# Attention and two feed-forward layers in one kernel: the conversion of w_in started earlier, cut into two steps and spread over more units

## The chip, the cores and the metric

One core of a Trainium2 chip runs the whole kernel. The metric is the device time of one execution in microseconds (us). Five engines work side by side, each through its own queue, strictly in order: PE (TensorE: matrix products and transposes), ACT (ScalarE), DVE (VectorE), POOL (GpSimd) and SP (here only the issuer of most transfers). An engine that waits for something holds everything that is queued behind it.

## The reference

```python
def _attn_ref(q, k, v, f):                      # q, k, v: (4, 8, 576, 64); f: (4, 8, 576)
    scores = scale * np.matmul(q, k.transpose(0, 1, 3, 2))
    cum = np.cumsum(np.log(np.clip(f, 0.0001, 1.0)), axis=-1)
    decay = cum[:, :, :, None] - cum[:, :, None, :]
    scores = np.where(causal, -1000000000.0, scores + decay)
    attn = softmax(scores)                      # with 1e-09 added to the sum
    return np.matmul(attn, v)

def _moe_ref(x, w_in, w_out):                   # w_in: 512 x 2048, w_out: 2048 x 512
    h = x @ w_in
    g = h * np.tanh(softplus(h))
    return g @ w_out

def _moe2_ref(x, w1, w2, w3, w_out):
    h = np.maximum(np.maximum(x @ w1, x @ w2), x @ w3)
    return h @ w_out

def reference(**kwargs):
    x = attn_out.transpose(0, 2, 1, 3).reshape(2304, 512)
    return _moe2_ref(_moe_ref(x, ...), ...)
```

The weights come as 64-bit floats; the kernel reads them as pairs of 32-bit words and makes 32-bit floats of them.

## The kernel before

**Attention.** The 32 heads are worked in 16 pairs, four to a batch element, counted here from 0 (pair 6 is the third of the second batch element). Each pair is cut into two units by rows of queries: unit 0 holds the rows 0 to 255, unit 1 the rows 256 to 575. `load` (L256) lets SP fetch q, k and the decay rows of a pair, two pairs ahead; `prep` (L304) turns q and k on PE (`tr`, L315 and L316) and copies them out of PSUM on ACT (`kT`, `qT`, `q`, L317 to L320); POOL masks the decay rows (`cb`, L298 and L302). `scores` (L341) multiplies on PE (`sc`, L339), adds the decay and finds the row minimum on DVE (`P<-sc`, L393, with `mn`), exponentiates on ACT (L399) and scales each row by its sum: the reciprocal on DVE (`rr`, L360 and L361), the product on POOL (L363). `av` (L407) runs two units later: PE turns P (`pp`, L438), ACT and DVE copy it out in turn (`TA`, `TB`, L442 and L444), PE multiplies with v (L418), and `split` writes the result as a high half `xh` (ACT, L134) and a low half `xl` (DVE, L140). The banks of PSUM for `tr` and `pp` are three in all (tag `ps`), so a bank that waits to be copied out holds back the next `pp`.

**w_in.** `load_w_in` (L201) makes the weights of the first feed-forward layer ready while attention runs. It has 16 chunks of 256 x 256, numbered here 0 to 15; two make one of the eight tiles `wi`. For a chunk SP fetches 512 KB into `wr` (L149; four buffers), and `convert` (L154) runs five steps on it: the absolute value of the upper word on ACT (`wt<-wr`, L159), a clip on POOL (`wt<-wt`, L163), and three steps on DVE (L166, L169, L173), of which the last two read `wr` again. `split` then writes the high half on ACT (`wi<-wt`, L134) and the low half on POOL (`wi<-wt,wi`, L140). `wt` has two buffers.

**What sets the order.** The program is written as generators that a main loop (from L540 on) advances one unit at a time; a scheduler then orders the instructions of each engine by priority and by times it estimates. Attention stands under `tc.high_priority(AHEAD)` with AHEAD = 3000; the conversion has no such rank and fills gaps. `queued(last)` holds an instruction behind another on its queue. In the main loop `na` counts units, and this line says how many steps of the conversion follow each:

```python
for _ in range(2 if 2 <= na <= 9 else na == 1):
    next(wgen, None)
```

The first step only fetches; after it, two chunks follow each of the units 2 to 9.

**The products with w_in.** `h_steps` (L505) multiplies blocks of 512 tokens with a `wi` (`h`, L184 to L186: three matmuls for each product, hi by hi, hi by lo, lo by hi). It has the lowest rank and is what PE does between the pieces of attention. After attention the second weight matrix and the second layer follow; the change does not touch them.

Of the kernel before, what the change touches and what calls it, by code (L numbers as in the profile page):

```python
# [12 lines left out]
I32 = mybir.dt.int32  # L13
AF = mybir.ActivationFunctionType
ALU = mybir.AluOpType
# [10 lines left out]
F32_MIN_AS_HIGH_HALF = struct.unpack("<f", struct.pack("<I", 0x38100000))[0]  # L26
F32_MAX_AS_HIGH_HALF = struct.unpack("<f", struct.pack("<I", 0x47EFFFFF))[0]
# [5 lines left out]
BLK = 256  # L33
BLK2 = 512
LEAD = 2
EDGE = 352


# [27 lines left out]
def tile_decay_attention__mish_ff__max3_ff(  # L66
# [16 lines left out]
    nc = tc.nc  # L83
# [10 lines left out]
    edge = ctx.enter_context(tc.tile_pool(name="edge", bufs=1, side="right"))  # L94
    edge.tile([128, EDGE // 4], F32, name="edge")
    at = ExitStack()
# [35 lines left out]
    def split(dst_hi, dst_lo, src, eng_hi, eng_lo):  # L132
        if eng_hi == "act":
            nc.scalar.activation(dst_hi, src, AF.Copy)  # L134
        elif eng_hi == "pool":
            nc.gpsimd.tensor_scalar(dst_hi, src, 1.0, 1.0, op0=ALU.mult, op1=ALU.mult)
        else:
            nc.vector.tensor_copy(dst_hi, src)
        eng = nc.gpsimd if eng_lo == "pool" else nc.vector
        return eng.tensor_tensor(out=dst_lo, in0=src, in1=dst_hi, op=ALU.subtract)  # L140

    pace, on_act, on_dve = [], [], []

    def fetch(pool, src, bufs):

        m, n = src.shape[0] // 128, src.shape[1]
        r = pool.tile([128, m, n, 2], I32, name="wr", tag="wr", bufs=bufs)
        with queued(pace):
            nc.sync.dma_start(  # L149
                r.rearrange("p m n w -> p m (n w)"), src.bitcast(I32).rearrange("(m p) w -> p m w", p=128)  # L150
            )
        return r

    def convert(pool, r, bufs=None, abs_eng="dve"):  # L154

        t = pool.tile([128, r.shape[1], r.shape[2]], F32, name="wt", tag="wt", bufs=bufs)
        lo, hi, ti = r[:, :, :, 0], r[:, :, :, 1], t.bitcast(I32)
        if abs_eng == "act":
            nc.scalar.activation(t, hi.bitcast(F32), AF.Abs)  # L159
        else:  # L160
            nc.vector.tensor_scalar(ti, hi, 0x7FFFFFFF, None, op0=ALU.bitwise_and)
        eng = nc.gpsimd if abs_eng == "act" else nc.vector
        eng.tensor_scalar(  # L163
            t, t, F32_MIN_AS_HIGH_HALF, F32_MAX_AS_HIGH_HALF, op0=ALU.max, op1=ALU.min
        )
        nc.vector.tensor_scalar(  # L166
            ti, ti, 3, 0x3FFFFFF8, op0=ALU.logical_shift_left, op1=ALU.bitwise_and
        )
        nc.vector.scalar_tensor_tensor(  # L169
            out=ti, in0=hi, scalar=-0x40000000, in1=ti,  # L170
            op0=ALU.bitwise_and, op1=ALU.bitwise_or,
        )
        nc.vector.scalar_tensor_tensor(  # L173
            out=ti, in0=lo, scalar=29, in1=ti,
            op0=ALU.logical_shift_right, op1=ALU.bitwise_or,
        )
        return t

    def queued(last):
        return tc.issue_after(last[-1].ins) if last else ExitStack()  # L180
# [15 lines left out]
    wst = top.enter_context(tc.tile_pool(name="wst", bufs=2))  # L196
# [3 lines left out]

    def load_w_in():  # L201
        jobs = [(fp, c) for fp in range(NFP) for c in range(0, KD, 2)]
        raws = []
        for k, (fp, c) in enumerate(jobs):
            for f_, c_ in jobs[len(raws):k + 3]:
                raws.append(fetch(wst, moe_w_in[c_ * 128:(c_ + 2) * 128, f_ * 256:f_ * 256 + 256], 4))
            if k == 0:
                yield
            t = convert(wst, raws[k], abs_eng="act")
            split(wi[fp][:, 0, c:c + 2], wi[fp][:, 1, c:c + 2], t, "act", "pool")  # L210
            if c + 2 == KD:
                loaded.add(fp)
            yield

    x = {}
# [25 lines left out]
    raws = [[ap_.tile([128, 640], F32, name=f"raw{c}{i}") for c in "qk"] for i in range(2)]  # L241
# [99 lines left out]
    def scores(J, g):  # L341


        P = {}
        u = count["unit"]
        count["unit"] += 1
        sm = sums[u % 4]
        mn = aw.tile([128, 6], F32, name="mn", bufs=4)
        rr = aw.tile([128, 5], F32, name="rr", bufs=4)
        tiles = [(h, qt) for qt in ((0, 1) if g == 0 else (2, 3)) for h in range(2)]  # L350
        if g == 1:
            tiles.append((None, 4))
        made = []
        col = 0

        def scale_rows(part):

            cs = slice(part[0], part[-1] + 1)
            with tc.high_priority(400):
                nc.vector.tensor_scalar(rr[:, cs], sm[:, cs], 1e-9, None, op0=ALU.add)  # L360
                nc.vector.reciprocal(rr[:, cs], rr[:, cs])  # L361
                for ci in part:
                    nc.gpsimd.tensor_scalar(made[ci], made[ci], rr[:, ci:ci + 1], 1.0, op0=ALU.mult, op1=ALU.mult)  # L363

        for ci, (h, qt) in enumerate(tiles):
            wd = (qt + 1) * 128 if qt < 4 else S
            Pt = aw.tile([128, wd], F32, name=f"P{qt}_{h}", bufs=LEAD)
            made.append(Pt)
            if h is None:
                P[4] = Pt  # L370
            else:
                P[h, qt] = Pt
            cb = decay(J, h, qt)
            if h is None:
                cb = [cb[:, n:n + 1] for n in range(2)]
            else:
                cb = [cb]
            s0 = 128 if qt == 1 else 0
            if not h and qt != 1:
                count["sc"] += 1  # L380
                pair = (aps if count["sc"] % 2 or not eps else eps[0]).tile([128, 2, 512], F32, name="sc", bufs=1)
                for n in range(2):
                    if h is None:
                        score_mm(J, h, qt, pair[:, n, :288], 288 * n, 288)
                    else:
                        score_mm(J, n, qt, pair[:, n, :wd], 0, wd)
                if qt == 0:
                    for n in range(2):
                        score_mm(J, n, 1, pair[:, n, 128:384], 0, 256)
            for pi, (c0, w) in enumerate([(0, wd)] if qt < 4 else [(0, 288), (288, 288)]):  # L390
                sc = pair[:, h or pi, s0:s0 + w]
                like = lambda t: t.rearrange("p (a c) -> p a c", a=cb[pi].shape[1])
                nc.vector.tensor_tensor_reduce(  # L393
                    out=like(Pt[:, c0:c0 + w]), in0=like(sc), in1=cb[pi],
                    scale=-scale, scalar=(3e38 if pi == 0 else mn[:, col - 1:col]),
                    op0=ALU.add, op1=ALU.min, accum_out=mn[:, col:col + 1],
                )
                col += 1
            nc.scalar.activation(  # L399
                Pt, Pt, AF.Exp, scale=-1.0, bias=mn[:, col - 1:col], accum_out=sm[:, ci:ci + 1],  # L400
            )
            if ci == 1:
                scale_rows([0, 1])
        scale_rows(list(range(2, len(tiles))))
        return P

# [54 lines left out]
    def attention():  # L461
# [9 lines left out]
        pend = []  # L471
        for n in range(len(units) + LEAD):
            if n == 6 + LEAD:
                eps.clear()
                early.close()
                eps_h.append(sa.enter_context(tc.tile_pool(name="hps", bufs=2, space=PSUM, reuse_waits="tile")))
            if n < len(units):
                ji, g = units[n]
                pend.append((J[ji], g, scores(J[ji], g)))
            if n >= LEAD:  # L480
                unit = pend.pop(0)
# [5 lines left out]
            if n < len(units) and g == (ji == 0) and ji + 1 < len(jobs):  # L487
                prep(J[ji + 1])
            if n >= LEAD:
                next(rest, None)  # L490
# [14 lines left out]
    def h_steps():  # L505
# [3 lines left out]
        for i, j in order:  # L509
# [28 lines left out]
            yield i  # L538

    wgen = load_w_in()  # L540
    attn = attention()
    steps = h_steps()
    credit, na = 0.0, 0
    while True:

        with tc.high_priority(AHEAD):
            done = next(attn, None)
        if done is None:
            break

        na += 1
        for _ in range(2 if 2 <= na <= 9 else na == 1):
            next(wgen, None)
        if len(loaded) == NFP and not x4:
            top.close()
            x4.append(top.enter_context(tc.tile_pool(name="x4", bufs=1)))
            x4[0].tile([128, (864 - EDGE) // 4], F32, name="gap")
        credit += RATE
        while credit >= 1.0:
            credit -= 1.0  # L560
            if next(steps, None) is None:
                credit = 0.0
# [274 lines left out]
    for t0 in (BLK2, BLK2 + 2 * HALF):  # L837
        hh = [hp2.tile([128, 2 * HALF], F32R, name=f"hh{c}") for c in range(NF2)]
        hl = [hp2.tile([128, 2 * HALF], F32R, name=f"hl{c}") for c in range(NF2)]
        for p in range(3):  # L840
            fs = slice(p * 128, p * 128 + 128)
            for m in range(3):
                S = []
                for k in range(4):
                    t = sst.tile([128, 2, 2, 128], F32R, name="s")
# [88 lines left out]
```

## Time and profile before

| what | value |
|---|---|
| median of 3 runs | 902.48 us (902.36 to 904.47) |
| the profiled execution's own time | 902.15 us |
| its span | 900.4 us |
| mean granted TensorE clock | 0.992 of 2.4 GHz |
| busy: PE, DVE, ACT, POOL | 97%, 56%, 45%, 26% of the span |

Shares of the span hide that the stages differ. The profile cuts the span into 40 slices of 22.5 us: POOL is busy for 8 to 9 tenths in the slices 3 to 5 and again for 8 tenths in slice 7, and for 3 tenths or less from slice 8 on. PE is at 9 tenths or more from slice 7 to slice 39. A row of the timeline gives the start, the length, the engine, the line, the operation and, in brackets, how long the engine sat idle before it and what ended that. Lines (L163) are those of the kernel before.

### The profile page before, as it was taken

The numbers are of one execution on the slowest core, as the hardware profiler recorded it, in microseconds if no ns is written. First come the engines' busy times: TensorE is split into PE (matmuls) and PEld (weight loads), VectorE is DVE, ScalarE is ACT, GpSimd is POOL, SyncE is SP. The second block draws the span as 40 slices with busy tenths as digits, with TensorE's granted clock in tenths as the row PEclk, the third lists the DMA queues.
The fourth block names the chain that finished last, engine by engine and source line by source line (L and its number), as shares of the span: only waits on it lengthen the run. The fifth ranks groups of instructions, "written<-read, shape, count | busy, mean of one in ns | idle before, by whom it ended". The sixth has DMA issues, their size and how long they took to land.

```text
span 900.4 us, 13933 instructions
## 1 busy us (share of the span) xinstructions
PE 873.3 (97%) x4800; PEld 704.8 (78%) x4800; DVE 504.9 (56%) x1186; ACT 401.7 (45%) x913; POOL 231.6 (26%) x317
## 2 busy tenths in 40 slices
PE   6898989999999999999999999999999999999998
PEld 3565756777777777889888888889888999889986
DVE  3688676354544433991367566675865556524540
ACT  4687656555555432443464455453433223312211
POOL 3689968333222210000020000000121323013310
PEclk8989999999999999999999999999999999999999
DMA  7886654444433115863456666673499443334401
GB/s 184 227 220 178 198 164 128 123 127 119 125 113 86 59 59 178 284 229 128 136 182 210 224 201 217 205 240 104 160 364 324 144 139 106 123 94 129 131 27 65
DMA packets 125030, 145.25 MB, mean 161 GB/s; under 512 B 64736, under 2 KB 78048, under 8 KB 124960
## 3 DMA queue, kind: packets, MB, share of 16 engines
q1 hardware_dynamic: 105856, 102.41, 38.9%
q10 hardware_dynamic: 16416, 27.79, 8.3%
q0 software_dynamic: 2688, 14.16, 4.3%
q8 instruction: 38, 0.62, 0.3%
q14 instruction: 32, 0.26, 0.1%
HBM read 102.83 MB, written 41.49 MB: 160 GB/s over the span
## 4 chain that ended last, share of the span: by engine, by line
PE 88%; POOL 3%; DMA 3%; DVE 2%; ACT 2%; issue 2%; SPq 1%; ACTq 0%; POOLq 0%; DVEq 0%
PE y L184 7%; PE y L185 7%; PE y L186 7%; PE h L184 6%; PE h L186 6%; PE h L185 6%; PE q L185 6%; PE q L186 6%; PE q L184 6%; PE sc L339 6%; PE av L418 4%; PE pp L438 4%; PE o L184 3%; PE o L185 3%; PE o L186 3%; PE g L184 2%
## 5 line engine op out<-in xcount | busy, mean ns | idle before, releaser
L184 PE MATMUL h<-xh,wi 128*128 128x512 f32 (+1 forms) x320 | 122.0, 383 | 0.6 <-DVE he L528 0.4
L185 PE MATMUL h<-xl,wi 128*128 128x512 f32 (+1 forms) x320 | 120.1, 375 | 1.8 <-DVE xl L140 1.8
L186 PE MATMUL h<-xh,wi 128*128 128x512 f32 (+1 forms) x320 | 120.1, 375 | 0.0
L185 PE MATMUL y<-gl,wo 128*128 128x512 f32 (+1 forms) x320 | 117.7, 368 | 0.0
L186 PE MATMUL y<-gh,wo 128*128 128x512 f32 (+1 forms) x320 | 117.5, 368 | 0.0
L184 PE MATMUL y<-gh,wo 128*128 128x512 f32 (+1 forms) x320 | 106.4, 369 | 0.0
L668 DVE TENSOR_TENSOR gl<-g,gh 128x512 fp32r<-128x512 f32 x72 | 49.9, 695 | 86.3 <-ACT gh L667 86.2
L363 POOL TENSOR_SCALAR P<-P,rr 128x128 f32<-128x128 f32 (+3 forms) x128 | 73.7, 589 | 85.1 <-DVE rr L361 51.2
L399 ACT ACTIVATE P<-P,mn 128x128 f32<-128x128 f32 (+3 forms) x128 | 70.6, 553 | 40.0 <-DVE mn L393 39.9
L661 ACT ACTIVATE g<-g 128x512 f32<-128x512 f32 x72 | 45.4, 633 | 88.7 <-DMA g<-h_d 85.7
L184 PEld LDWEIGHTS h<-xh,wi 128*128 128x128 f32 x320 | 60.2, 189 | 17.4 <-issue 3.2
L185 PEld LDWEIGHTS h<-xl,wi 128*128 128x128 f32 x320 | 60.4, 189 | 13.5 <-DVE xl L140 2.2
L186 PEld LDWEIGHTS h<-xh,wi 128*128 128x128 f32 x320 | 60.4, 189 | 11.4 <-issue 1.8
L185 PEld LDWEIGHTS y<-gl,wo 128*128 128x128 f32 x320 | 60.3, 189 | 10.1
L184 PEld LDWEIGHTS y<-gh,wo 128*128 128x128 f32 x320 | 60.2, 188 | 10.1
L186 PEld LDWEIGHTS y<-gh,wo 128*128 128x128 f32 x320 | 60.2, 188 | 10.0
L339 PE MATMUL sc<-kT,qT 64*128 64x128 f32 (+3 forms) x256 | 51.0, 500 | 4.4 <-DVE mn L393 4.0
L860 DVE TENSOR_TENSOR u<-q,p 128x448 f32<-128x448 f32 x36 | 22.4, 621 | 58.1 <-PE q L186 58.1
L438 PE MATMUL pp<-ident,P 128*128 128x128 f32 x320 | 49.7, 284 | 4.3 <-ACT qT L317 3.9
L531 ACT ACTIVATE he<-h 128x512 f32<-128x512 f32 x56 | 33.2, 593 | 44.6 <-PE h L186 41.5
L438 PEld LDWEIGHTS pp<-ident,P 128*128 128x128 f32 x320 | 37.2, 143 | 20.0 <-issue 5.8
L667 ACT ACTIVATE gh<-g 128x512 fp32r<-128x512 f32 x72 | 44.4, 620 | 9.4 <-PE y L186 8.9
(141 smaller groups left out, 1846.4 us busy)
## 6 DMA issues: line engine op xcount, KB each, us to landing
g<-h_d SPq DMA_DIRECT2D x72, 256.0 KB, 3.1
s<-s_d SPq DMA_DIRECT2D x72, 256.0 KB, 2.9
h_d<-he ACTq DMA_DIRECT2D x56, 256.0 KB, 2.8
wr<-in_moe_w_out_dram SPq DMA_DIRECT2D x22, 512.0 KB, 4.6
wr<-in_moe_w_dram SPq DMA_DIRECT2D x24, 384.0 KB, 3.8
s_d<-sk POOLq DMA_DIRECT2D x12, 768.0 KB, 5.8
cb<-cum_d SPq DMA_DIRECT2D x32, 256.0 KB, 4.1
wr<-in_moe_w_in_dram SPq DMA_DIRECT2D x16, 512.0 KB, 4.2
```

The source lines that it names most:

```text
L184: nc.tensor.matmul(ps, wh, xh, start=start, stop=False, skip_group_check=True)
L185: nc.tensor.matmul(ps, wh, xl, start=False, stop=False, skip_group_check=True)
L186: return nc.tensor.matmul(ps, wl, xh, start=False, stop=stop, skip_group_check=True)
L339: nc.tensor.matmul(dst, lhs, J["k"][rows, c0:c0 + w], start=True, stop=True, skip_group_check=True)
L363: nc.gpsimd.tensor_scalar(made[ci], made[ci], rr[:, ci:ci + 1], 1.0, op0=ALU.mult, op1=ALU.mult)
L399: nc.scalar.activation(Pt, Pt, AF.Exp, scale=-1.0, bias=mn[:, col - 1:col], accum_out=sm[:, ci:ci + 1],)
L418: last = nc.tensor.matmul(acc[(U, L)[h], off:off + w], J["vs"][:, n * 64:n * 64 + 64], T[:, at[h]:at[h] + w], start=(kt, off) == first, st ...
L438: turn = nc.tensor.transpose(pp[:, n * 128:n * 128 + 128], Pt[:, k0:k0 + 128], ident)
L531: nc.scalar.activation(he, h, AF.Copy)
L661: nc.scalar.activation(g, g, AF.Mish)
L667: on_act[:] = [nc.scalar.activation(gh, g, AF.Copy)]
L668: on_dve[:] = [nc.vector.tensor_tensor(out=gl, in0=g, in1=gh, op=ALU.subtract)]
```

## The change

`convert` is cut into two: `convert` now ends after the clip when the absolute value is on ACT, and a new `join` holds the three steps on DVE. `load_w_in` keeps a list `begun`: a step of the generator starts chunk k (absolute value, clip) and then finishes chunk k - 1 (`rest`: join, split). The clip is held behind the last scaling of a unit so far (`on_scale`), the join behind the last score of a unit so far (`on_score`). The first fetch gets the rank 2950, just below attention. The steps are spread anew: the fetch follows unit 1, nothing follows unit 2, and one step follows each of the units 3 to 18.

```diff
+LAG = 1
...
         eng = nc.gpsimd if abs_eng == "act" else nc.vector
-        eng.tensor_scalar(
-            t, t, F32_MIN_AS_HIGH_HALF, F32_MAX_AS_HIGH_HALF, op0=ALU.max, op1=ALU.min
-        )
+        with queued(on_scale if abs_eng == "act" else []):
+            eng.tensor_scalar(
+                t, t, F32_MIN_AS_HIGH_HALF, F32_MAX_AS_HIGH_HALF, op0=ALU.max, op1=ALU.min
+            )
+        return t if abs_eng == "act" else join(r, t)
+
+    def join(r, t):
+
+        lo, hi, ti = r[:, :, :, 0], r[:, :, :, 1], t.bitcast(I32)
...
     def load_w_in():
         jobs = [(fp, c) for fp in range(NFP) for c in range(0, KD, 2)]
-        raws = []
-        for k, (fp, c) in enumerate(jobs):
-            for f_, c_ in jobs[len(raws):k + 3]:
-                raws.append(fetch(wst, moe_w_in[c_ * 128:(c_ + 2) * 128, f_ * 256:f_ * 256 + 256], 4))
-            if k == 0:
-                yield
-            t = convert(wst, raws[k], abs_eng="act")
+        raws, begun = [], []
+
+        def rest(k, r, t):
+            fp, c = jobs[k]
+            with queued(on_score):
+                join(r, t)
             split(wi[fp][:, 0, c:c + 2], wi[fp][:, 1, c:c + 2], t, "act", "pool")
             if c + 2 == KD:
                 loaded.add(fp)
+
+        for k in range(len(jobs)):
+            for f_, c_ in jobs[len(raws):k + 3]:
+                with tc.high_priority(2950) if len(raws) < 1 else ExitStack():
+                    raws.append(fetch(wst, moe_w_in[c_ * 128:(c_ + 2) * 128, f_ * 256:f_ * 256 + 256], 4))
+            if k == 0:
+                yield
+            begun.append((k, raws[k], convert(wst, raws[k], abs_eng="act")))
+            if len(begun) > LAG:
+                rest(*begun.pop(0))
+            yield
+        while begun:
+            rest(*begun.pop(0))
             yield
...
-                    nc.gpsimd.tensor_scalar(made[ci], made[ci], rr[:, ci:ci + 1], 1.0, op0=ALU.mult, op1=ALU.mult)
+                    on_scale[:] = [nc.gpsimd.tensor_scalar(made[ci], made[ci], rr[:, ci:ci + 1], 1.0, op0=ALU.mult, op1=ALU.mult)]
...
-                nc.vector.tensor_tensor_reduce(
+                score = nc.vector.tensor_tensor_reduce(
...
+            if ci == len(tiles) - 1:
+                on_score[:] = [score]
...
-        for _ in range(2 if 2 <= na <= 9 else na == 1):
+        for _ in range((0,1,0,1,1,1,1,1,1,1,1,1,1,1,1,1,1,1,1)[na] if na < 19 else 0):
             next(wgen, None)
```

No instruction is added or removed in the conversion itself; what changes is where each stands on its queue. Three places matter below. In the names `wr` and `wt` are the raw and the converted chunk, `P_0` and `P_1` the two heads' probabilities, numbers at the end only tell tiles apart.

The first is ACT's queue where the conversion begins. Before, with chunk 0 and chunk 1:

```order
L317 ACTIVATE kT<-tr 128x512
L399 ACTIVATE P_0_728,sums_176<-P_0_728,mn 128x384
L159 ACTIVATE wt<-wr 128x512
L399 ACTIVATE P_1_734,sums_176<-P_1_734,mn 128x384
L159 ACTIVATE wt<-wr 128x512
L317 ACTIVATE qT<-tr 128x512
L318 ACTIVATE kT<-tr 128x64
L320 ACTIVATE q_1_193<-tr 64x64 x2
L134 ACTIVATE xh_450<-av 128x256
```

Now, with the two absolute values of chunk 1 and chunk 2 (chunk 0 stands 16 rows earlier, and its high half is the first row here):

```order
L135 ACTIVATE wi_152<-wt 128x512
L418 ACTIVATE P_0_663,sums_176<-P_0_663,mn 128x384
L465 ACTIVATE TA<-pp 128x512
L418 ACTIVATE P_1_669,sums_176<-P_1_669,mn 128x384
L336 ACTIVATE kT<-tr 128x512
L160 ACTIVATE wt<-wr 128x512
L135 ACTIVATE xh_415<-av 128x256
L418 ACTIVATE P_0_676,sums_176<-P_0_676,mn 128x512
L160 ACTIVATE wt<-wr 128x512
L418 ACTIVATE P_1_682,sums_176<-P_1_682,mn 128x512
L337 ACTIVATE kT<-tr 128x64
L339 ACTIVATE q_1_193<-tr 64x64 x2
```

So two absolute values stand here as before, now those of the second and third transfer, and the copies `kT` 128x64 and `q` stand behind both.

The second is SP's queue at the loads of the third pair (pair 2), now:

```order
L280 DMA rawq_179<-in_q_dram 128x4x64 x2
L284 DMA rawq_179<-in_q_dram 64x2x64
L294 DMA cb<-cum_d 128x2x256
L150 DMA wr<-in_moe_w_in_dram 128x2x512
L294 DMA cb<-cum_d 128x2x256
L297 DMA cb_367<-cum_d 64x576 x2
```

Before, four fetches of w_in stood together after the loads of pair 4 (`DMA wr<-in_moe_w_in_dram 128x2x512 x4`). Now one stands here, and a group of four, the transfers of chunks 1 to 4, stands where the group stood.

The third is DVE's queue in pair 6, from the scores of 384 columns to those of 512. Before:

```order
L166 TENSOR_SCALAR wt<-wt 128x512
L140 TENSOR_TENSOR xl_1473<-av,xh_1472 128x128
L169 SCALAR_TENSOR_TENSOR wt<-wr,wt 128x512
L173 SCALAR_TENSOR_TENSOR wt<-wr,wt 128x512
L393 ISA P_0_1631,mn<-sc,cb 128x384
...
L166 TENSOR_SCALAR wt<-wt 128x512
...
L361 RECIPROCAL rr<-rr 128x2
L140 TENSOR_TENSOR xl_594<-av,xh_593 128x256
L166 TENSOR_SCALAR wt<-wt 128x512
L169 SCALAR_TENSOR_TENSOR wt<-wr,wt 128x512
L393 ISA P_0_1644,mn<-sc,cb 128x512
```

Now:

```order
L176 SCALAR_TENSOR_TENSOR wt<-wr,wt 128x512
L141 TENSOR_TENSOR xl_1407<-av,xh_1406 128x128
L180 SCALAR_TENSOR_TENSOR wt<-wr,wt 128x512
L412 ISA P_0_1585,mn<-sc,cb 128x384
...
L379 TENSOR_SCALAR rr<-sums_176 128x2
L380 RECIPROCAL rr<-rr 128x2
L141 TENSOR_TENSOR xl_549<-av,xh_548 128x256
L412 ISA P_0_1598,mn<-sc,cb 128x512
```

One chunk's steps still stand ahead of the scores of 384 columns; the two that stood between those and the scores of 512 columns are gone from there.

## Rows read from the trace of the kernel before

**Rows 1.** Windows: stretch, length, busy PE, PEld, DVE, ACT, POOL (instructions), clock, DMA share, GB/s.
```profile
67.50:90.00 22.50, 19.23 (x169) 13.13 (x165) 19.00 (x51) 15.94 (x46) 21.14 (x22) 1.00 0.65 178
90.00:112.50 22.50, 22.26 (x145) 16.01 (x141) 14.82 (x41) 13.85 (x36) 21.46 (x25) 1.00 0.68 199
112.50:135.00 22.50, 18.10 (x122) 13.11 (x123) 17.49 (x34) 12.89 (x30) 15.67 (x14) 1.00 0.53 163
135.00:157.50 22.50, 21.22 (x118) 15.11 (x115) 14.59 (x44) 14.02 (x38) 18.45 (x21) 1.00 0.45 129
157.50:180.00 22.50, 22.50 (x146) 15.99 (x146) 8.93 (x37) 11.50 (x33) 6.82 (x14) 1.00 0.40 123
```

**Rows 2.** PE's timeline on both sides of its longest wait in attention.
```profile
40.97 0.60 PE L438 MATMUL pp<-ident,P 128*128 128x128 f32 x4
45.48 1.11 PE L438 MATMUL pp<-ident,P 128*128 128x128 f32 x4 [3.90 <-ACT qT L317]
```

**Rows 3.** ACT's timeline over the same stretch.
```profile
41.85 0.66 ACT L159 ACTIVATE wt<-wr 128x512 f32<-128x512 f32 x1 [3.42 <-DMA wr<-in_moe_w_in_dram]
42.42 0.60 ACT L399 ACTIVATE P<-P,mn 128x384 f32<-128x384 f32 x1
...
44.27 0.67 ACT L159 ACTIVATE wt<-wr 128x512 f32<-128x512 f32 x1 [1.16 <-DMA wr<-in_moe_w_in_dram]
...
45.42 0.45 ACT L320 ACTIVATE q<-tr 64x64 f32<-64x64 f32 x2
45.89 0.38 ACT L134 ACTIVATE xh<-av 128x256 fp32r<-128x256 f32 x1
46.17 0.71 ACT L399 ACTIVATE P<-P,mn 128x512 f32<-128x512 f32 x1
```

**Rows 4.** The chain that ended last, from 36 to 46 us: start, length, what.
```profile
37.62 6.63 DMA wr<-in_moe_w_in_dram
```

**Rows 5.** SP's timeline: the last load of pair 2's q, and the first of w_in.
```profile
20.82 0.61 SPq L265 DMA_DIRECT2D rawq<-in_q_dram  x1
...
36.99 2.63 SPq L149 DMA_DIRECT2D wr<-in_moe_w_in_dram  x4
```

**Rows 6.** The tile wr: its 16 transfers, from issue to landing.
```profile
DMA to landing us min/median/max: 3.6/4.2/7.9
```

**Rows 7.** PE's window with the low clock, columns as in rows 1, PE alone.
```profile
45.20:52.00 6.80, 6.53 (x27) 0.50 0.91 223
```

**Rows 8.** PE's waits from 100 to 157 us: total us, times, longest.
```profile
PE sc L339 <- DVE mn L393: 4.9, 4, 2.1
PE av L418 <- ACT TB L444: 0.8, 1, 0.8
```

**Rows 9.** PE's timeline, the two longest of those waits.
```profile
115.86 1.13 PE L339 MATMUL sc<-kT,qT 64*128 64x512 f32 x4 [1.49 <-DVE mn L393]
...
124.48 0.75 PE L339 MATMUL sc<-kT,q 128*128 128x288 f32 x2 [2.11 <-DVE mn L393]
```

**Rows 10.** DVE's timeline ahead of them.
```profile
112.40 0.83 DVE L166 TENSOR_SCALAR wt<-wt 128x512 int32<-128x512 int32 x1 [2.00 <-POOL wt L163]
...
114.68 0.55 DVE L393 CUSTOM_DVE_ANT_0 P<-sc,cb 128x384 f32<-128x384 f32 x1
...
121.30 1.18 DVE L166 TENSOR_SCALAR wt<-wt 128x512 int32<-128x512 int32 x1
122.51 0.69 DVE L169 SCALAR_TENSOR_TENSOR wt<-wr,wt 128x512 int32<-128x512 int32 x1
123.12 0.68 DVE L393 CUSTOM_DVE_ANT_1 P<-sc,cb 128x512 f32<-128x512 f32 x1
```

**Rows 11.** POOL's timeline in pair 6: four scalings, two clips, one low half.
```profile
108.75 1.62 POOL L363 TENSOR_SCALAR P<-P,rr 128x128 f32<-128x128 f32 x4
110.45 3.81 POOL L163 TENSOR_SCALAR wt<-wt 128x512 f32<-128x512 f32 x2
115.50 1.27 POOL L140 TENSOR_TENSOR wi<-wt,wi 128x512 fp32r<-128x512 f32 x1 [1.25 <-ACT wi L134]
```

More of the change, by code (lines that the diff above doesn't have):

```diff
@@ L140, in split @@
         return eng.tensor_tensor(out=dst_lo, in0=src, in1=dst_hi, op=ALU.subtract)
-    pace, on_act, on_dve = [], [], []
+    pace, on_act, on_dve, on_score, on_scale = [], [], [], [], []
     def fetch(pool, src, bufs):
```

## The prediction

> **What bounds the kernel now.** I read the windows first. From 157.5 us on PE is busy without a gap (22.50 of 22.50) while POOL has fallen to 6.82 [rows 1]; ahead of that, while w_in is converted, PE lacks 3.27 us in 67.5 to 90, 0.24, 4.40 and 1.28 us in the next three stretches, and POOL works 21.14, 21.46, 15.67 and 18.45 of each 22.50 us [rows 1]. So the end is set by PE, and what the change can win is PE's idle time in the stretch in which attention and the conversion share the engines. PE's work itself stays the same.
>
> Then PE's timeline: the longest wait in attention is 3.90 us, up to 45.48, and was ended by ACT's copy `qT` [rows 2]. ACT's timeline says why ACT was late: it stood 3.42 us until 41.85 and 1.16 us until 44.27 at the absolute values of chunks 0 and 1, for their transfers [rows 3]. The chain of waits runs through the same place: 6.63 us of the transfer that lands at 44.25 [rows 4]. Behind that wait PE's granted clock is 0.50, its lower level of 1.2 GHz, from 45.2 to 52.0 us, with 6.53 us of work in it [rows 7]; at 2.4 GHz this work would be about half, so the spell costs some 3.3 us more.
>
> Then PE's waits from 100 to 157 us: 4.9 us in four waits for scores to be read by DVE, and one of 0.8 us for a copy of P [rows 8]. The two longest are 1.49 and 2.11 us [rows 9]. On DVE the scores of 384 columns at 114.68 stood behind a step that had waited 2.00 us for POOL's clip, and those of 512 columns at 123.12 behind two more steps, 1.18 and 0.69 us long [rows 10]. The clip in question ran on POOL from 110.45, two in a row of 3.81 us, right behind the four scalings from 108.75 [rows 11].
>
> The sum is made against the profiled execution's own 902.15 us; the median of the runs shown is 902.48, 0.33 us higher, a tenth of what a measurement of this kernel can tell from no change (about 0.3%, 2.7 us).
>
> **The change part by part.**
>
> *A. The wait at 41.6 us.* The first transfer leaves earlier. In the new order of SP it stands behind the last load of q of pair 2, which before went out at 20.82 [rows 5], with three v loads and one decay row now ahead of it; at some 0.66 us an issue (2.63 for four [rows 5]) that is five issues later, 24.1 us. With the median landing of 4.2 us [rows 6] it lands at 28.3. But ACT's place at 38 us still holds two absolute values, now of the second and third transfer, and these go out in a group of four where the old group stood, one issue later: 37.6 and 38.2 us. Before, the first two of the group landed 4.86 us after the first issue (41.85, [rows 3]) and at 44.25 [rows 4]. Moved by one issue: 42.4 and 44.9. On ACT then: absolute value to 42.97 (0.57 from start to start), `xh` 0.28, the exponential of 512 columns 0.70, the second absolute value from 44.9 to 45.5, another exponential 0.70, `kT` 128x64 0.10 and `q` 0.45 [rows 3]. In the new order PE's `pp` waits for the bank that `q` frees, not for `qT`: 46.8 instead of 45.48, **+1.3 us**. If the clock comes back at 52.0 as before, 1.3 us less run at half rate, which gives 0.65 back; I take **+0.7**. Bounds: with the shortest landing of 3.6 us for both [rows 6] the same steps end at 44.6, -0.9; with the longest of 7.9 us for the third transfer at 47.9, +2.4.
>
> The Trainium skill, "DMA: Bandwidth & Descriptors", section "Anatomy of one DMA", fits a transfer to about 2.0 us and its bytes over 436 GB/s, which by my estimate is 3.2 us for 512 KB; no landing in the trace is that short. The page gives the fit for the path that GpSimd issues, and these go by SP. By it, this part would come out as -1.3 us and the sum as 896.9, if transfers that leave together share nothing.
>
> *B. What chunk 0 adds ahead of that.* Its absolute value, clip, three DVE steps and split now run between 28 and 37 us. PE's next pieces there are fed by work of ACT and DVE that is done, so I take 0. If DVE's three steps delay the scores in full it is +2.2 us (0.83 and twice 0.69 [rows 10]); a gain has no source here, since nothing is taken away from this stretch.
>
> *C. Pairs 3 to 5 (57 to 108 us).* The order has the same number of low halves on POOL in these pairs and one clip more. POOL stays as full as it was [rows 1], so I take 0, between -3.3 and +3.3, PE's idle time in 67.5 to 90 [rows 1] saved or once more.
>
> *D. Pair 6 (108 to 140 us).* Five chunks were finished here, now two. The clip ahead of the scores of 384 columns now stands behind two scalings instead of four, half of 1.62 us [rows 11]: the wait of 1.49 shrinks by 0.8. The two chunks' steps between the scores of 384 and those of 512 columns are gone from DVE: the wait of 2.11 goes whole. Of the other 2.1 us (4.9 and 0.8 less 1.49 and 2.11 [rows 8, 9]), which lie behind the same steps later on, I take 1.3. What is late next is PE's own queue, which has `h` products to fill with. **-4.2 us**; bounds 0 and -5.7, all of it.
>
> *E. Chunks 12 to 15, now beside pairs 7 and 8.* POOL is idle for two thirds of the time there [rows 1], so their 4 x (1.9 + 1.27) us [rows 11] are hidden if they come in time: PE's `h` products with the last two `wi` follow their low halves by a few us in the new order. I take +0.3; if one chunk is late by a clip and a low half, +3.2.
>
> *F. The first rank, the holding behind scores and scaling, the list `begun`* change only where these instructions stand, which A to E have counted. SP issues the same number of transfers; the v loads of pair 2 go out 1.7 us sooner and the decay rows 0.6 us later, with the masks on POOL moved behind two more scalings: 0.
>
> Sum: 0.7 + 0 + 0 - 4.2 + 0.3 = -3.2 us: 902.15 - 3.2 = **899.0 us**, 0.35% faster.
>
> **The rivals.**
>
> *Rival 1, faster by more: the transfers of chunks 1 and 2 land sooner than their forerunners.* Less is queued ahead of them, the first having gone. If both land in the shortest time of the trace, 3.6 us [rows 6], A is -0.9 and the time 902.15 - 0.9 - 4.2 + 0.3 = 897.4. At the far end they land before ACT asks (before, it asked at 38.4, 41.85 less 3.42 [rows 3]); then A is -3.9 [rows 2] and -3.3 for the clock [rows 7], and the time 891.1. Against: the group of four still leaves within 2.6 us [rows 5]. Chance 0.12, most of it near the first figure.
>
> *Rival 2, no change: what D saves is lost to another wait.* One chunk's steps still stand ahead of the scores of 384 columns, and behind them on DVE the copies that PE waits for. If POOL's clip remains the last to end (as in [rows 10]), D gives only its 0.8, and the time is 902.15 + 0.7 - 0.8 + 0.3 = 902.4. For it: 4.9 of 5.7 us of these waits are DVE's, whatever stood ahead. Chance 0.27.
>
> *Rival 3, slower: late chunks hold PE in pairs 7 and 8.* Before, all chunks were done by pair 7; now the last four come one a unit, each just ahead of the `h` product that reads it. PE is in order, so a late low half stops attention too. It decides from the point at which a low half is written later than PE's ninth matmul on that `wi`. Two chunks late by a clip and a low half each cost 6.4 us [rows 11]; with D and A that is 902.15 + 0.7 - 4.2 + 6.4 = 905.1, and with D down to its 0.8, 908.5. Against: POOL is at a third there. Chance 0.16.
>
> **How the numbers follow.** The forecast has 0.45, the rivals 0.12, 0.27 and 0.16. The range reaches from 894.5 (the forecast with all of D and the better bound of A, 902.15 - 0.9 - 5.7 - 1.0; a third of rival 1 lies below) to 904.5 (rival 2 with the worse bound of A, 902.4 - 0.7 + 2.4 = 904.1, and a little of E; most of rival 3 is left out): it leaves about 0.08 below and 0.12 above. The forecast alone would reach from 896 to 902. Faster by over 0.3% (below 899.8): most of rival 1, two thirds of the forecast, since B, C and A can each take 0.5 us from a sum that lies 0.8 us beyond the bound, and a little of rival 2: 0.47. Slower by over 0.3% (above 905.2): a part of rival 3 and of the worse bounds of A and B: 0.17. Between: 0.36.
>
> **What would show it.** In the profile of the changed kernel: two waits of ACT for `wr` at 39 to 45 us and PE's `pp` behind them ended by ACT `q`, at about 46.8 (A); the granted clock at 0.50 behind it up to some 52 us; none of PE's waits for DVE over 1 us between 108 and 140 us of the old time (D); PE without a gap beside pairs 7 and 8 (E). The prediction is wrong if ACT does not stand for transfers 2 and 3 (rival 1), if waits for DVE in pair 6 add up to over 3 us (rival 2), or if PE waits for a `wi` (rival 3).

## The result, and the profile after

The changed kernel takes 907.75 us (median of four runs, 906.70 to 908.58) where the kernel before, timed beside it, takes 902.42: a ratio of 1.0062, 95% interval 1.0047 to 1.0077. It is slower by twice what a measurement can tell from no change, and lies outside the predicted range. The profiled execution takes 906.7 us (span 904.6).

I read the windows first, as for the kernel before. Ahead of the five of [rows 1] stand here the first 67.5 us, before and after. The columns are those of [rows 1]. Before:

```profile
0.00:42.00 42.00, 32.52 (x179) 18.81 (x179) 21.53 (x90) 23.24 (x70) 19.49 (x51) 0.92 0.76 194
42.00:67.50 25.50, 22.02 (x142) 14.89 (x142) 20.39 (x70) 20.54 (x61) 22.43 (x29) 0.87 0.86 237
```

After:

```profile
0.00:42.00 42.00, 30.20 (x171) 17.72 (x171) 23.40 (x93) 24.59 (x73) 21.80 (x49) 1.00 0.78 208
42.00:67.50 25.50, 21.96 (x150) 14.96 (x150) 20.16 (x69) 19.61 (x59) 23.74 (x30) 0.87 0.78 209
67.50:90.00 22.50, 19.35 (x130) 13.68 (x132) 17.54 (x48) 14.43 (x42) 19.52 (x23) 0.85 0.66 173
90.00:112.50 22.50, 21.45 (x166) 15.14 (x167) 15.25 (x44) 13.91 (x38) 19.87 (x22) 1.00 0.72 203
112.50:135.00 22.50, 21.78 (x127) 15.42 (x129) 11.53 (x38) 13.31 (x35) 13.71 (x16) 1.00 0.60 173
135.00:157.50 22.50, 22.50 (x135) 15.50 (x133) 12.02 (x36) 12.81 (x33) 9.23 (x14) 1.00 0.41 125
157.50:180.00 22.50, 20.56 (x130) 14.73 (x125) 14.21 (x38) 13.47 (x37) 16.42 (x20) 1.00 0.39 107
```

PE's idle time is the length less the busy time. It grows by 2.3 us up to 42 us, stays as it was to 67.5, changes by -0.1 and +0.8 in the next two stretches, falls by 3.7 and 1.3 from 112.5 to 157.5, and grows by 1.9 behind that. The sum to 180 us is 22.1 us before and 22.2 after. Behind attention the two run alike: the first product `y` starts at 421.4 us before and at 426.0 after. So the change won idle time where it was meant to and lost as much elsewhere; **the whole loss lies in PE's busy time**, 877.8 us against 873.3 by the pages of the profile, for the same 4800 records of matmuls. Two things stretch it.

**The clock.** These are windows of PE alone (length, busy, clock, DMA share, GB/s):

```profile
45.90:53.20 7.30, 6.48 (x29) 0.53 0.77 189
77.00:83.80 6.80, 5.56 (x18) 0.50 0.71 166
```

The first answers to [rows 7]. The second, at 1.2 GHz, does not stand in the trace before: 5.56 us of work, 2.8 us of it lost if half the time is enough at 2.4 GHz. It is not the changed kernel's alone, though. Experiment 8 has the order of the kernel before on every engine up to 144 us, and its trace has such a spell near 82 us (last section). So 2.8 us is what this one trace shows, and cannot be called a price of the change.

**The order.** PE's timeline after, at the places that matter:

```profile
42.80 0.38 PE L334 MATMUL tr<-ident,rawq 128*128 128x128 f32 x2
46.72 1.12 PE L459 MATMUL pp<-ident,P 128*128 128x128 f32 x4 [3.54 <-ACT q L339]
...
74.91 0.66 PE L459 MATMUL pp<-ident,P 128*128 128x128 f32 x4
78.24 2.29 PE L358 MATMUL sc<-kT,q 128*128 128x288 f32 x4 [2.67 <-DVE mn L412]
...
143.41 1.12 PE L358 MATMUL sc<-kT,qT 64*128 64x512 f32 x2
144.46 0.65 PE L439 MATMUL av<-TA,vs 128*64 128x256 f32 x2
145.03 1.12 PE L358 MATMUL sc<-kT,qT 64*128 64x512 f32 x2
...
172.59 0.50 PE L191 MATMUL h<-xh,wi 128*128 128x512 f32 x1 [1.94 <-ACT he L552]
...
182.25 0.48 PE L358 MATMUL sc<-kT,qT 64*128 64x128 f32 x2
182.67 0.33 PE L439 MATMUL av<-TB,vs 128*64 128x64 f32 x2
182.93 0.49 PE L358 MATMUL sc<-kT,qT 64*128 64x128 f32 x2
```

And before, at the scores that answer to those at 143 and 182 us:

```profile
144.17 1.13 PE L339 MATMUL sc<-kT,qT 64*128 64x512 f32 x4 [0.48 <-DVE mn L393]
145.23 0.65 PE L418 MATMUL av<-TA,vs 128*64 128x256 f32 x4
...
178.62 0.93 PE L339 MATMUL sc<-kT,qT 64*128 64x128 f32 x8
```

Each program matmul leaves two records here, so x4 is the scores of 512 columns of both heads (each head's use 64 of the array's 128 rows, `64*128`). Right behind each other they take 1.06 us together (144.17 to 145.23). With an `av` between them, each head's takes as long alone: 1.05 us (143.41 to 144.46) and the same again. The `av` products of the two heads lose in the same way: x4 took 0.58 us before (to the `pp` at 145.81), x2 now takes 0.57. From the start of the `av` group to the next `pp` this piece takes 3.48 us after, and 1.86 in experiment 1 below, where nothing is parted: 1.6 us. The same stands in pair 6 at 118.55 us. In pair 9 the four score matmuls are parted three times: 5.13 us for scores and `av` (181.65 to 186.78) where before they took 0.85 and 2.25, so 2.0 us. Together some 5.2 us, more than the whole loss. The order of PE had it, before any run; in pair 6 of the changed program:

```
L439 MATMUL av<-TA,vs_185 64x256
L358 MATMUL sc<-kT,qT 128x512
L439 MATMUL av<-TA,vs_185 64x256
L358 MATMUL sc<-kT,qT 128x512
```

The Trainium skill, "TensorEngine Tiling (Array Packing)", section "Key Properties", says that different tiles of the array can execute their matmuls in parallel, and that a change of the tiling mode drains TensorE. The trace agrees with the first (two matmuls of 64 rows in 1.06 us); no run here prices the drain by itself.

ACT at the start of the conversion (it answers to [rows 3]):

```profile
28.41 0.68 ACT L160 ACTIVATE wt<-wr 128x512 f32<-128x512 f32 x1 [0.68 <-DMA wr<-in_moe_w_in_dram]
...
43.33 0.66 ACT L160 ACTIVATE wt<-wr 128x512 f32<-128x512 f32 x1 [1.87 <-DMA wr<-in_moe_w_in_dram]
...
44.86 0.66 ACT L160 ACTIVATE wt<-wr 128x512 f32<-128x512 f32 x1
...
46.22 0.45 ACT L339 ACTIVATE q<-tr 64x64 f32<-64x64 f32 x2
```

DVE ahead of PE's new wait at 75.6 us:

```profile
76.54 0.43 DVE L173 TENSOR_SCALAR wt<-wt 128x512 int32<-128x512 int32 x1 [2.55 <-POOL wt L165]
76.88 0.68 DVE L412 CUSTOM_DVE_ANT_1 P<-sc,cb 128x512 f32<-128x512 f32 x1
...
77.49 0.69 DVE L412 CUSTOM_DVE_ANT_1 P<-sc,cb 128x512 f32<-128x512 f32 x1
```

POOL over the same time:

```profile
71.97 2.54 POOL L382 TENSOR_SCALAR P<-P,rr 128x128 f32<-128x128 f32 x4
74.59 1.91 POOL L165 TENSOR_SCALAR wt<-wt 128x512 f32<-128x512 f32 x1
```

The first join step of chunk 5 stands on DVE ahead of the scores of 512 columns of pair 4, which PE had written by 73.1. It waits for the chunk's clip, and the clip stands behind four scalings. Before, the scores of this pair were read at 72.88, ahead of the steps of the next chunk. It is the pattern that the change took out of pair 6 [rows 10, 11], now in pair 4.

### The profile page after: what moved, and what is told of

Its sections match the earlier page's. It is cut to its first block, busy times and chain, and to the rows that moved or that the text cites. A ratio compares the mean times of both kernels' runs of the same rounds, so it can differ in the third digit from the quotient of the medians.

```text
span 904.6 us, 13920 instructions
## 1 busy us (share of the span) xinstructions
PE 877.8 (97%) x4800; PEld 707.9 (78%) x4800; DVE 502.4 (56%) x1186; ACT 405.1 (45%) x913; POOL 231.5 (26%) x317
## 4 chain that ended last, share of the span: by engine, by line
PE 90%; POOL 2%; DMA 2%; ACT 2%; DVE 2%; issue 1%; SPq 1%; POOLq 0%; DVEq 0%
PE y L191 7%; PE y L192 7%; PE y L193 7%; PE h L191 7%; PE h L193 7%; PE h L192 7%; PE sc L358 6%; PE q L192 6%; PE q L191 6%; PE q L193 6%; PE av L439 5%; PE pp L459 4%; PE o L191 3%; PE o L192 3%; PE o L193 3%; PE g L191 2%
## 5 line engine op out<-in xcount | busy, mean ns | idle before, releaser
L358 PE MATMUL sc<-kT,qT 64*128 64x128 f32 (+3 forms) x256 | 53.4, 493 | 1.2 <-DVE mn L412 0.7
```

What stands on the lines that cost most here:

```text
L358: nc.tensor.matmul(dst, lhs, J["k"][rows, c0:c0 + w], start=True, stop=True, skip_group_check=True)
```

## The experiments

Three theories. **P**: the parted pairs cost 4 to 5 us. **R**: the rank of the first transfer, which pulls chunk 0 and all behind it forward, makes the waits up to 42 us and the one at 75.6. **H**: the holding is what freed pair 6. The rival to P, called W, puts the loss in waits and clock alone. Times are medians of fresh runs beside the kernel before (901.99 to 902.68 us in these); ratios are to it, with 95% intervals.

**1. Two parted pairs joined.** The second half of `av` goes ahead of the scores; no other engine's order changes.

```diff
-                        score_mm(J, n, qt, pair[:, n, :wd], 0, wd)
+                        with queued(last_av if (u, qt) in ((13, 3), (15, 3)) else []):
+                            score_mm(J, n, qt, pair[:, n, :wd], 0, wd)
```

> Theory P (parted pairs): in the changed kernel the two heads' score matmuls, which run at once when one stands right behind the other (64x512, four records in 1.06 us), are parted by av products at three places, so each takes as long alone (1.03 us) as both together. At two of them (scores of 512 columns of pairs 6 and 7) the trace shows 2.09 us for the scores and 1.14 for the four av records instead of 1.06 and 0.58: 1.3 to 1.6 us each. This kernel joins these two pairs again and changes nothing else in any engine's order: 907.75 - 2.6 = 905.1 us, and a 64x512 x4 group of 1.06 us near 119 and 143 us. Theory W (the loss is all waits and clock: PE's idle time early, the wait near 76 us with the low clock behind it, and the one near 171 us): nothing moves, 907.75 within 0.8.

Measured: 904.71 us, 1.0025 (1.0009 to 1.0042), so by the ratios 0.37% or 3.3 us less than the changed kernel (3.0 by the medians). PE's line groups to 360 us, the scores and `av` from TA, of the changed kernel:

```profile
L358 PE MATMUL sc<-kT,qT 64*128 64x128 f32 (+3 forms) x256 | 53.4, 493 | 1.2 <-DVE mn L412 0.7 <-ACT qT L336 0.4
L439 PE MATMUL av<-TA,vs 128*64 128x256 f32 (+1 forms) x128 | 16.1, 353 | 0.0
```

and of this one:

```profile
L358 PE MATMUL sc<-kT,qT 64*128 64x128 f32 (+3 forms) x256 | 51.1, 492 | 1.4 <-DVE mn L413 0.9 <-ACT qT L336 0.4
L440 PE MATMUL av<-TA,vs 128*64 128x256 f32 (+1 forms) x128 | 14.8, 352 | 0.0
```

2.3 and 1.3 us less busy, for the same matmuls. P holds, with 1.6 us for each place, the upper of the two prices that I had given.

**2. Without the rank**, the rest kept.

```diff
-                with tc.high_priority(2950) if len(raws) < 1 else ExitStack():
+                with ExitStack():
```

> The rank of the first transfer taken back, the rest of the change kept. Theory R: the rank pulls chunk 0 and all behind it forward, which puts the join step of chunk 5 ahead of the scores of 512 columns of pair 4 on DVE (here they stand ahead of it again) and chunk 0's work into the stretch before 42 us. Then PE's wait of 2.67 us near 76 us, the low clock behind it (2.6 us) and the extra 2.7 us of waits before 42 us are gone, and of the parted pairs two are left (2.3 us instead of 4.4): 907.75 - 2.67 - 2.6 - 2.7 - 2.1 = 897.7 us. Rival: the waits come from the spread and the steps themselves and only change place: 907.75 - 2.1 = 905.7.

Measured: 901.77 us, 0.9992 (0.9981 to 1.0003). Better than the rival's 905.7, not as good as 897.7: the wait at 75.6 is gone, but two low-clock spells stand at 44.5 to 48.5 and 78.5 to 82.5 us, and in pairs 7 and 10 scores are parted.

**3. Without the two holdings.**

```diff
-        with queued(on_scale if abs_eng == "act" else []):
+        with ExitStack():
...
-            with queued(on_score):
+            with ExitStack():
```

> Both holdings (clip behind scaling, join behind score) taken away, the rest of the change kept. Up to pair 5 no engine's order changes; from there chunks 12 to 15 come one to two units sooner, with the steps of two of them among the scores of pair 6 again. Theory H (the holding is what saved pair 6 and what delayed the last chunks): waits of PE for DVE of 2 to 4.9 us come back between 108 and 145 us, the wait of 1.94 us near 171 us goes, and the parted scores of pair 9 (1.8 us) too: 907.75 + 3.4 - 1.9 - 1.8 = 907.5, between 906 and 909. Rival (the holding does nothing for pair 6, the wider spread does): 907.75 - 3.7 = 904.0.

Measured: 905.84 us, 1.0041 (1.0023 to 1.0060), between the two. Pair 9 is no longer parted and the wait near 171 us is gone, while near 117 and 144 us there are waits of only 1.0 us (0.72 in the changed kernel) and 0.95. With the rank in place this does not settle H; experiments 5 and 7 do.

**4. All score pairs joined.**

```diff
+                        with queued(one), tc.high_priority(3 * AHEAD) if one else ExitStack():
+                            one = [score_mm(J, n, qt, pair[:, n, :wd], 0, wd)]
```

> Every score matmul of the second head is put right behind that of the first (held behind it, with a high rank), in the whole kernel. Theory P: no pair is parted, 907.75 - 4.4 = 903.4 us, with PE's busy time about 4.4 us less than the changed kernel's 877.8; other orders move a little in pairs 1 to 8, so within 2 us. The wait near 76 us may shrink, since the scores of 512 columns of pair 4 stand one step later on DVE. Theory W: 907.75 within 1.5, with PE's busy time as before.

Measured: 903.58 us, 1.0014 (1.0002 to 1.0026), with PE busy for 872.0 us. As P had it, by its own order, although its waits up to 430 us (23.1 us) are longer than the changed kernel's (22.1).

**5 to 7. Rank and holding apart, with nothing parted.** From pair 6 on (`u >= 13`) the two heads' scores are joined as in 4; 5 has no rank, 6 is the same with the rank, 7 is 5 without the holdings.

```diff
-                with tc.high_priority(2950) if len(raws) < 1 else ExitStack():
+                with ExitStack():
...
+                        with queued(one), tc.high_priority(3 * AHEAD) if one and u >= 13 else ExitStack():
+                            one = [score_mm(J, n, qt, pair[:, n, :wd], 0, wd)]
```

> The kernel without the rank (901.77 us, still with two parted score pairs, near 139 us and in pair 10) with the score matmuls of the two heads put one right behind the other from pair 6 on; up to pair 7 no engine's order moves else. Theory P: the 2.3 us of these two pairs go, 901.77 - 2.3 = 899.4 us, 0.4% below the kernel before (902.7), and this is then what the spread, the steps and the holding are worth by themselves. Theory W: 901.8.

> The same as the kernel beside it (no parted score pair from pair 6 on), but with the rank of the first transfer: the two differ by the rank alone. Theory R: the rank costs PE's wait of 2.67 us for the scores of pair 4 with a low clock behind it (1.7 to 2.6 us), and up to 2.7 us of waits before 42 us; 899.4 + 4.2 = 903.6 us or some more. Rival (the rank is free; taking it back only helped because the order it gave parted more pairs): 899.4 as the kernel beside it.

> The kernel without the rank and without parted pairs, and also without the two holdings: what is left of the change is the cut into two steps and the new spread. On DVE the order of the scores and the conversion's steps is then that of the kernel before from pair 3 to pair 7 (the steps of chunk 11 ahead of the scores of 512 columns of pair 6). Theory H (the holding alone moved the steps off pair 6): PE's waits of 5 us from 108 to 145 us are back but for 1 us, 899.4 + 4 = 903.4, between 902 and 904. Rival (the spread or the lag does it): 899.4.

Measured: 5: 899.50 us, 0.9970 (0.9956 to 0.9984). 6: 903.31, 1.0016 (1.0000 to 1.0032). 7: 901.38, 0.9994 (0.9980 to 1.0007). PE's waits from 60 to 180 us (total us, times, longest), of 5:

```profile
PE h L192 <- DVE xl L141: 1.8, 1, 1.8
PE sc L358 <- DVE mn L415: 1.8, 2, 1.5
```

of 6:

```profile
PE sc L358 <- DVE mn L415: 3.7, 2, 2.7
PE h L191 <- ACT he L555: 2.2, 1, 2.2
```

of 7:

```profile
PE sc L358 <- DVE mn L415: 7.4, 5, 2.1
PE h L192 <- DVE xl L141: 1.8, 1, 1.8
```

5 against 6: the rank costs 0.46%, 4.2 us (3.8 by the medians); the 2.7 us are the wait in pair 4, the 2.2 that of the last chunks, and both go with it. The other half of R, the waits up to 42 us, these traces do not show: PE is idle there for 10.6 us in 5 and 11.1 in 6. 7 against 5: the holding is worth 0.24%, 2.2 us (1.9 by the medians); without it the waits for scores are back as before (6.1 us in this stretch). I had expected 4. So the cut into two steps and the new spread by themselves change nothing that can be told (7), the holding wins 2, the rank loses 4, and the parted pairs lose another 4: 1.0062 less 1.0016 of 6, which has the changed kernel's order on ACT, POOL and SP, and another at 19 of 4800 places on PE and 7 of 1186 on DVE.

**8. The kernel before with two pairs parted.**

```diff
+                        with queued(last_av if n and qt == 3 and u > 11 else []):
+                            score_mm(J, n, qt, pair[:, n, :wd], 0, wd)
```

> The kernel before, with the second head's scores of 512 columns parted from the first's by one other matmul in two places (near 145 and 168 us; from pair 6 on they are held behind the last av product). Theory P: 1.0 us each, 902.7 + 2.0 = 904.7 us, and at these places two groups of two records of 64x512 of about 1.0 us each instead of one of four in 1.06. Theory W: 902.7, since all the matmuls are the same.

Measured: 904.31 us, 1.0026 (1.0011 to 1.0042): 2.3 us, against the 2.0 of P and none of W. Its timeline:

```profile
145.39 1.09 PE L339 MATMUL sc<-kT,qT 64*128 64x512 f32 x2 [0.48 <-DVE mn L394]
146.42 0.65 PE L419 MATMUL av<-TA,vs 128*64 128x256 f32 x4
147.00 1.12 PE L339 MATMUL sc<-kT,qT 64*128 64x512 f32 x2
```

**9 to 12. Taking ACT's stand for the transfers away, on kernel 5.** The absolute values are held behind a copy of the pair made ready last (`q` in 9 and 10, `qT` in 11 and 12), and the chunks are handed out later: the diff is that of 12, without what it shares with 5; 9 has the same list, in 10 the three twos stand at the places 5 to 7, and in 11 the first chunk at place 6 with one a unit.

```diff
+            with queued(on_prep):
+                nc.scalar.activation(t, hi.bitcast(F32), AF.Abs)
...
+            on_prep[:] = [nc.scalar.activation(dst[:, 0:512], tr, AF.Copy)]
...
-        for _ in range((0,1,0,1,1,1,1,1,1,1,1,1,1,1,1,1,1,1,1)[na] if na < 19 else 0):
+        for _ in range((0,1,0,0,0,0,2,2,1,1,1,1,1,1,1,1,1,1,1,1)[na] if na < 20 else 0):
```

> On the kernel of 899.5 us (no rank, no parted pairs): every absolute value is held on ACT behind the last copy q of the pair made ready last, and the first chunks are handed out four units later, two at a time. Theory A (ACT standing for a transfer, with the copies that PE's pp waits for behind it, is what costs PE 2.8 to 4.7 us near 45 us and a low clock of 1.7 to 3.4 us behind it): this wait goes, and of the low clock near 46 us nothing is left: 899.5 - 3.5 - 1.7 = 894.3. But the order puts the steps of chunk 4 ahead of the scores of 512 columns of pair 4 again (as the rank did): 2.7 us and a low clock of 1.7 back: 898.7 us; and without the wait's going 903.9. Rival (the wait near 45 us covers a time in which PE would lack other work anyway): 903 to 904.

> The same holding of the absolute values, with the first chunks handed out one unit sooner; on DVE the steps of two chunks stand ahead of the scores of 512 columns of pair 4, behind a clip that has four scalings ahead of it, and those of chunk 11 ahead of the 288-column scores of pair 6. Theory A: as beside it, 3.5 to 5.2 us off near 45 us, 2.7 to 4.4 on near 76 us, 1 on in pair 6: between 898 and 901 us. Rival: 902 to 905.

> On the kernel of 899.5 us: each absolute value is held on ACT behind the copy qT of the pair made ready last, and the chunks are handed out from the sixth step on, one a unit. On ACT the first absolute value then stands behind kT, q and qT of pair 3, so that a late transfer holds none of them. Theory A (ACT standing for the transfers is what makes PE wait 2.8 to 4.7 us near 45 us): that wait goes, with the low clock behind it (1.7 us): 899.5 - 3.5 - 1.7 = 894.3. The chunks come later; in pair 7 the steps of two of them stand ahead of the scores of 512 columns (up to 2.5 us): between 894 and 897. Rival (the wait there is not ACT's alone: POOL, DVE or the loads end it at nearly the same time): 899 to 902.

> The same holding with the chunks handed out two a unit at first, as early as in the kernel of 899.5 us from the ninth step on. On ACT the first absolute value stands behind both copies q, but still ahead of qT of pair 3. Theory A: PE waits only for qT, about as long as the transfer is late (3 us at 39.1 us in the kernel with the copies q ahead), so half of the wait at most goes: 897.5 to 900. On DVE no step of a chunk stands ahead of the scores of pair 6, and one chunk's ahead of the scores of 512 columns of pair 4. Rival: 900 to 903.

Measured: 9: 904.18 us, 1.0018 (1.0003 to 1.0033). 10: 905.01, 1.0032 (1.0020 to 1.0045). 11: 904.15, 1.0025 (1.0016 to 1.0034). 12: 899.22, 0.9970 (0.9958 to 0.9982). In 9 the copies `q` went ahead, but `qT` stayed behind the absolute values, and PE waited for it:

```profile
46.69 2.93 PE L359 MATMUL sc<-kT,qT 64*128 64x128 f32 x12 [3.79 <-ACT qT L337]
```

In 9 and 10 the edit missed its aim, and join steps ahead of the scores of pair 4 cost 3.7 and 3.1 us once more. In 11 the long wait is gone too, but three shorter ones stand behind it (0.52, 0.73 and 1.34 us, to 49.97) with a low clock from 49 to 56 us, and three more to 152.91 us (1.62, 0.79, 1.50) with one from 151 to 159. In 12 the wait is gone, and from 20 to 225 us no stretch shows a low clock:

```profile
41.85 1.57 PE L359 MATMUL sc<-kT,qT 64*128 64x128 f32 x12 [0.40 <-ACT qT L337]
```

Yet 12 is no faster than 5: waits of 1.0 to 2.0 us for `wi`, TB and `xl` stand in its place, and the idle time up to 430 us is 21.5 us against 19.4. So theory A is right about the wait and wrong about its worth. Kernels 5 and 12 beat the kernel before by 0.3% and the changed one by 0.9%.

## Why the prediction was wrong

**"PE's work itself stays the same."** This sentence of the first part failed, and with it the 0 that the sum had for the rank of the first transfer (F). By the ratios of the runs the result of +5.6 us is the sum of three parts: -2.7 for what 5 keeps of the change, +4.2 for the rank (6 against 5), +4.2 for the parted pairs (the changed kernel against 6). I took PE's time as work plus waits and looked on PE only for waits. The work was the same, its time was not: three groups of scores were parted by `av`, some 5.2 us by the rows; joining them gave 3.3 us for two (1) and about 4.2 for nearly all (6). No term of the sum, bound or rival had it, though the order of PE shows it.

**A, +0.7: the mechanism and the times right, the price not shown.** The first transfer was awaited until 28.41 us (28.3 predicted; partly luck, since it left at 23.52 and not 24.1, and took 4.9 us and not 4.2), the second until 43.33 (42.4), the third had landed by 44.86 (44.9), and PE went on at 46.72 (46.8), released by ACT's `q`, with the clock low behind it to about 53. But PE came to this wait 1.6 us later than before, so the wait was not longer (3.54 us, 3.90 before), its idle time from 42 to 67.5 us stayed (3.48, now 3.54), and the clock was not back at 52.0. By the Trainium skill, "DMA: Bandwidth & Descriptors", section "Anatomy of one DMA", I had estimated 3.2 us for a transfer. The shortest of the sixteen takes 3.6 us, as before, and the second, which left in a group of four at 37.28, took 6.0. For those that leave together the estimate does not hold.

**B, 0: too low.** PE's idle time up to 42 us grew by 2.3 us, about the bound of 2.2 that I had named and set aside. Behind the start of chunk 0's work at 28.41 PE waits 0.88 us for POOL's P (at 35.40) and 0.45 and 0.78 us for DVE (39.84, 41.83). That PE's next pieces there are fed by work already done was wrong. How much this costs is open: traces with one and the same order up to 42 us differ there by nearly as much (11.8 us of idle time in the changed kernel, 11.4, 11.1 and 9.95 in 1, 6 and 3; 9.5 in the kernel before, 10.2 in 8).

**C, 0: too low.** From 67.5 to 112.5 us the idle time grew by 0.7 us (3.51 to 4.20), and the low clock of this trace costs some 2.8 more, together just beyond the bound of 3.3. I counted POOL's clips and low halves in these pairs, and not which join step stands ahead of which scores on DVE. That was the reading I had made for pair 6.

**D, -4.2: right.** From 112.5 to 157.5 us the idle time fell from 5.68 to 0.72 us, by 5.0. The waits of [rows 9] went but for 0.72. It is the holding that does it: without it (7 against 5) the waits for scores are back.

**E, +0.3: too low, inside its bound.** 1.94 us in pair 8. Not for a late `wi` as in rival 3: ACT's copy `he`, which frees PE's bank, stood behind a high half that waited 2.65 us for a join step.

**F, 0: failed.** "Change only where these instructions stand" was true of the conversion. Its places moved those of PE's own matmuls, and A to E had not counted what the rank does: 4.2 us by 6 against 5, with the wait of 2.67 us in pair 4 among them.

The forecast of 899.0 is near what the kernel gives without the rank and with nothing parted (899.5). That is no support for its sum: in that kernel the first transfer does not leave early, and PE's wait near 45 us, which A was about, is 4.7 us long. Of the rivals, 1 fell (ACT did stand for the transfers) and 2 fell (pair 6 lost nothing to another wait for DVE); 3 comes near the time, which is luck: its mechanism, a late low half that PE waits for, did not occur. Of the signs of being wrong that the prediction named none came: ACT stood for both transfers, pair 6 kept 0.72 us of waits for DVE, and PE waited for no `wi`. By the rows the terms come to more than the 4.5 us of the result: 5.2 parted, 2.8 of the low clock near 80 us, less about 0.6 us for an early one that costs less (see below) and less 0.2 of waits. PE's line groups up to 430 us give, after less before, +2.4 us for the scores of 64 rows, +1.3 for those of 288 columns, +1.5 for `av` from TA, +0.5 for `h` and -0.6 for `pp`. Where the remaining 2 to 3 us were won back I have not followed.

## What to carry to other kernels

Read the new order on the engine that sets the end as well as on those that it waits for: which neighbours ran at once, and whether they still are neighbours. Moving a background task earlier does not only move its cost; each step of it has to be looked up against the piece of the main work that is queued behind it. Try each part of such a change alone: here one part won 2 us, one lost 4, and a side effect lost 4. And before a short spell of low clock in one trace is put down to a change, look for it in a second trace with the same order.

## What the runs showed that I had not expected

- Two matmuls that use different halves of the array's rows ran at once as direct neighbours (1.06 us for both), and one after the other (1.05 us each) wherever another stood between. Parting two pairs in an otherwise equal kernel (8) cost 2.3 us.
- The record of the granted clock can miss a spell. After, it says 1.00 for 14.5 to 18.5 us, yet the scores of 288 columns take 2.29 us there, as at 0.50 before; before, the next scores of 512 columns took 2.08 us, after 1.16. So an early low clock is there in both. After, it ends sooner, and it also begins sooner: the four `tr` at 14.03 us take 1.09 us, where those at 14.02 took 0.64 before. Together these pieces take some 0.6 us less after:

```profile
16.68 2.29 PE L358 MATMUL sc<-kT,q 128*128 128x288 f32 x4
18.90 1.16 PE L358 MATMUL sc<-kT,qT 64*128 64x512 f32 x4
```

- A wait of the same length leaves a low clock in one kernel and none in another: PE waits 1.79 us up to 79.41 in kernel 5 and runs at 0.57 from 80.5 to 84.5; before, it waits 1.79 us up to 79.89 and runs at 1.00 from 80 to 84. Even the same order up to there does not settle it. In 8, which up to 144 us has the order of the kernel before on every engine, the same six `pp` behind the same wait take 1.48 us (granted clock 0.50 from 81 to 84 us), before 0.82 (1.00). First the kernel before, then 8:

```profile
79.89 0.50 PE L185 MATMUL h<-xl,wi 128*128 128x512 f32 x1 [1.79 <-DVE xl L140]
...
80.91 0.82 PE L438 MATMUL pp<-ident,P 128*128 128x128 f32 x6
...
80.45 0.62 PE L185 MATMUL h<-xl,wi 128*128 128x512 f32 x1 [1.80 <-DVE xl L140]
...
82.14 1.48 PE L439 MATMUL pp<-ident,P 128*128 128x128 f32 x6
```

A sum that puts a price on the clock behind a single wait is uncertain by that price.
